# Block-causal attention and a feed-forward on one core: the softmax constant added one column at a time

## The chip, the cores and the metric

The kernel runs on one core of one Trainium2 chip. The metric is the device time of one execution in microseconds. Before the change the median of three runs is 1260.88 us (1260.35 to 1262.1).

## The reference, cut to what matters

Eight batches of eight heads, 576 positions, head size 64. Attention with a mask over blocks of 64 positions, then a feed-forward on the 4608 rows of 512.

```python
def _attn_ref(q, k, v):
    scores = scale * np.matmul(q, k.transpose(0, 1, 3, 2))
    scores = np.where(block_i >= block_j, scores, -1000000000.0)
    scores = scores - np.max(scores, axis=-1, keepdims=True)
    attn = np.exp(scores)
    attn = attn / (np.sum(attn, axis=-1, keepdims=True) + 1e-09)
    return np.matmul(attn, v)

def _moe_ref(x, w_in, w_out):
    h = x @ w_in
    g = np.where(h >= 1, h, np.where(h <= -1, 0.0, (h + 1) ** 2 / 4))
    return g @ w_out
```

The change touches the `+ 1e-09` and the sum before it.

## The kernel before, in words

Two heads make a *pair*; there are 32 pairs, four to a batch. The 576 query positions of a head are four tiles of 128 rows and a rest of 64. `scores(j, g)` handles the query tiles of head j of the pair in three groups: group 0 holds two tiles (128 and 256 keys wide) in one PSUM bank, groups 1 and 2 one tile each (384 and 512 keys). `scores_last` handles the two rests of a pair together, as 128 rows of 576 keys in two halves of 288.

Each group goes through the same steps. TensorE makes the scores `ps_s` (L483, L486). VectorE takes the negative row maximum `nm` (L506). ScalarE takes the exponential into `pr` (L510), and an accumulator read that follows puts each row's sum into one column of `sm`. VectorE then adds EPS to the sums (L492), inverts them (L493), both in `inverse`, and scales `pr` by the result (L516). In group 0 `sm` has two columns, so L492 and L493 work on 128x2 values, elsewhere on 128x1. In `scores_last` the two halves' sums are added first (L540), then comes `inverse` on one column, then the scaling (L542). The scaled `pr` goes through a DMA on SyncE's queue into `prr` (L250; in the second batch into other buffers, L246, and in the first straight from `pr`) and is turned by TensorE (`turn`, `turn_last`: L553 and L555 into `ps_t`), cut into two words by ScalarE and VectorE (L546, L548), and multiplied with V (L592 into `ps_av`). From the third batch on, `add_words` puts that result together: ScalarE copies half of it into `xtmp` (L614), VectorE adds the other half into `x` (L615). The queries and keys of the next pair are turned by TensorE into `ps_qk` (L402, L443) and cut into words by ScalarE and VectorE (L389, L390, L395, L396, L447).

`ps_s`, `ps_t`, `ps_av` and `ps_qk` all take their PSUM bank from `work_bank`: three banks in turn once the feed-forward runs. A matmul into a fresh bank therefore waits until the last reader of the bank's tile three turns earlier is done.

The feed-forward runs a chunk of 512 rows behind the attention, interleaved with it: `ffn_in` (L771, 12 matmuls into `ph`, then ScalarE L780, VectorE L781 and L784, ScalarE L785, GpSimd L786, which makes `gl`) and `ffn_out` (L795, L800). GpSimd also makes the second words of V (L380), of `x` (L658) and, in the first part of the program, of the weights (L183, L187, an in-order list of conversions) and of the keys (L365).

The source gives a list of steps, and a scheduler of the framework lays each engine's instructions out in an order of its own from the dependences and its estimates of durations. Each engine then runs its list in order, and waits on semaphores of the others. A change of a few instructions can so change the order of others.

Of the kernel before, what the change touches and what calls it, by code (L numbers as in the profile page):

```python
# [11 lines left out]
ALU = mybir.AluOpType  # L12
# [11 lines left out]
def block_attn_then_ffn(  # L24
# [9 lines left out]
    nc = tc.nc  # L34
# [19 lines left out]
    EPS = 1e-9  # L54
# [22 lines left out]
    def work_bank(name):  # L77

        banks["n"] += 1
        if banks["free"] and banks["n"] % 2:  # L80
            return ps_o.tile([P, 512], F32, tag="po", name=name)
        return ps_w.tile([P, 512], F32, tag="work", name=name)
# [23 lines left out]
    def last_blocks(t_):  # L106
# [19 lines left out]
        out=msel[:NTL, : NTL * BLK].rearrange("p (t c) -> p t c", c=BLK),  # L126
# [106 lines left out]
    def as_float32r(src, plain):  # L233

        if plain:
            wide = src.shape[1] > RING - 2 * S
            places = SPARE_WIDE if wide else SPARE
            moved = [places[spare[wide] % len(places)]]
            spare[wide] += 1
            if src.shape[1] > TCH:  # L240
                if "end" not in spare:
                    spare["end"] = att1.tile([P, G0 + P], F32R, tag="pa11", name="pre")[:, :BLK]
                moved.append(spare["end"])
            for i, dst in enumerate(moved):
                n = min(TCH, src.shape[1] - i * TCH)
                nc.sync.dma_start(dst[:, :n].bitcast(F32), src[:, i * TCH : i * TCH + n])  # L246
            return moved
        n, moved = src.shape[1], []
        wide = wide_tile(F32R, "prr")
        nc.sync.dma_start(wide[:, :n].bitcast(F32), src)  # L250
        for c0 in range(0, n, TCH):
            moved.append(wide[:, c0 : min(c0 + TCH, n)])
        return moved


    class Pair:
# [232 lines left out]

        def inverse(self, total):  # L490

            nc.vector.tensor_scalar_add(total, total, EPS)  # L492
            nc.vector.reciprocal(total, total)  # L493

        def scores(self, j, g):
# [23 lines left out]
        def scores_last(self):  # L519

            half = S // 2
            pr = att3.tile([P, S], F32, tag="pr", name="pr")
            nm = small.tile([P, 3], F32, tag="nm", name="nm")
            sm = small.tile([P, 3], F32, tag="sm", name="sm")
            banks = []
            for i in range(2):
                ps = work_bank("ps_s")
                for j in range(2):
                    self.product(ps[:, :half], j, SM, i * half, half, j == 0, j == 1)
                nc.vector.tensor_reduce(  # L530
                    out=nm[:, i : i + 1], in_=ps[:, :half], axis=AX.X, op=ALU.max, negate=True
                )
                banks.append(ps)
            nc.vector.tensor_tensor(out=nm[:, 2:3], in0=nm[:, 0:1], in1=nm[:, 1:2], op=ALU.min)
            for i in range(2):
                nc.scalar.activation(
                    pr[:, i * half : (i + 1) * half], banks[i][:, :half], AF.Exp,
                    bias=nm[:, 2:3], scale=1.0, accum_out=sm[:, i : i + 1],
                )
            nc.vector.tensor_tensor(out=sm[:, 2:3], in0=sm[:, 0:1], in1=sm[:, 1:2], op=ALU.add)  # L540
            self.inverse(sm[:, 2:3])
            nc.vector.tensor_scalar_mul(pr, pr, sm[:, 2:3])  # L542
            self.pr["last"] = as_float32r(pr, self.plain) if self.hop else [pr]

# [341 lines left out]
```

## Time and profile before

| | us |
|---|---|
| median of the runs (1260.35 to 1262.1) | 1260.88 |
| span of the profiled execution, first to last instruction | 1262.2 |
| TensorE busy in the span | 1193.1 (95%) |
| VectorE busy | 888.1 (70%) |
| ScalarE busy | 695.3 (55%) |
| GpSimd busy | 375.3 (30%) |

The page gives for the profiled execution its span, and no other time of its own; it is 1.3 us above the median of the runs. The program has three parts: a start of about 265 us in which the weights are converted and the first two batches go through attention; a body from 265 to 1064 us in which 24 pairs follow each other every 33.5 us, with the feed-forward between them; and an end of 198 us of feed-forward alone. In the rows of the profile PE is TensorE's matmul, PEld its weight load, DVE VectorE, ACT ScalarE, POOL GpSimd and SP SyncE; a row of the timeline has the start, the duration, engine, line, operation, what it writes and reads, and in square brackets the idle time ahead of it and what ended that.

### The profile page before, as it was taken

To read this page: it belongs to the slowest core of one execution; us is meant where nothing else is said; L and a number is where in the kernel's file an instruction comes from. 1 tells how busy PE (TensorE), PEld (TensorE's weight loads), DVE (VectorE), ACT (ScalarE), POOL (GpSimd) and SP (SyncE) were. 2 spreads that over 40 slices of the span, in tenths; PEclk is the share of its full clock that TensorE was granted. 3 is DMA by queue.
4 is the path that set the end of the run, shared out by engine and by line. 5 is a ranking of instruction groups with operands and counts; after the bars stand their busy time and mean duration, and the time that the engine had idled before them with its cause. 6 is when DMAs were issued, how large, how long until landed. Compare 5 with 4: busy or idle time off the path is not lost.

```text
span 1262.2 us, 19823 instructions
## 1 busy us (share of the span) xinstructions
PE 1193.1 (95%) x6280; PEld 995.7 (79%) x6280; DVE 888.1 (70%) x2092; ACT 695.3 (55%) x1731; POOL 375.3 (30%) x366
## 2 busy tenths in 40 slices
PE   4887988999999999999999999999999999999998
PEld 3665876788888888888888888888888888888886
DVE  8888688658777877787777877787778776222322
ACT  5776666446565666565556565565656655222222
POOL 3444556312222222222222222222222222222222
PEclk9887999999999999999999999999999999999999
DMA  5566676778887654565555545554556433422432
GB/s 162 167 183 208 215 253 213 217 219 236 277 270 242 187 151 146 163 195 158 148 151 174 179 144 156 153 179 140 161 156 188 143 118 119 133 93 91 134 101 100
DMA packets 177191, 215.39 MB, mean 171 GB/s; under 512 B 109872, under 2 KB 128304, under 8 KB 176320
## 3 DMA queue, kind: packets, MB, share of 16 engines
q1 hardware_dynamic: 177088, 214.14, 55.3%
q8 instruction: 50, 0.82, 0.3%
q14 instruction: 53, 0.43, 0.1%
HBM read 134.74 MB, written 31.98 MB: 132 GB/s over the span
## 4 chain that ended last, share of the span: by engine, by line
PE 69%; DVE 17%; ACT 5%; issue 5%; DMA 3%; POOL 1%; SPq 0%; ACTq 0%; DVEq 0%; POOLq 0%
PE ph L771 27%; PE po L795 15%; PE po L800 8%; PE ps_av L592 8%; PE ps_s L483 4%; PE ps_s L486 3%; ACT pr L510 3%; PE ps_t L553 2%; DVE pr L516 2%; DVE t L781 2%; DVE pb L548 2%; DVE t L784 2%; ACT t L780 2%; DVE nm L506 2%; DVE sm L492 1%
## 5 line engine op out<-in xcount | busy, mean ns | idle before, releaser
L786 POOL TENSOR_TENSOR gl<-t,gh 128x512 fp32r<-128x512 f32 x144 | 186.1, 1292 | 530.9 <-ACT gh L785 360.6
L795 PE MATMUL po<-wo,gh 128*128 128x512 f32 x1152 | 295.2, 397 | 0.1
L795 PEld LDWEIGHTS po<-wo,gh 128*128 128x128 f32 x1152 | 211.9, 189 | 43.6 <-ACT gh L785 0.6
L771 PE MATMUL ph<-xh,wih 128*128 128x512 f32 x576 | 231.4, 402 | 4.7 <-DVE t L784 4.4
L771 PE MATMUL ph<-xh,wil 128*128 128x512 f32 x576 | 226.8, 394 | 0.0
L771 PE MATMUL ph<-xl,wih 128*128 128x512 f32 x576 | 226.1, 393 | 0.0
L781 DVE SCALAR_TENSOR_TENSOR t<-t 128x512 f32<-128x512 f32 x144 | 101.8, 707 | 162.6 <-ACT t L780 159.6
L510 ACT ACTIVATE pr<-ps_s,nm 128x128 f32<-128x128 f32 (+3 forms) x256 | 133.9, 526 | 83.8 <-DVE nm L506 81.2
L780 ACT ACTIVATE t<-ph 128x512 f32<-128x512 f32 x144 | 85.9, 597 | 158.1 <-PE ph L771 158.1
L785 ACT CAST gh<-t 128x512 fp32r<-128x512 f32 x144 | 89.5, 621 | 121.0 <-DVE t L784 120.7
L800 PE MATMUL po<-wo,gl 128*128 128x512 f32 x576 | 155.4, 392 | 0.0
L483 PE MATMUL ps_s<-ka,qa 68*128 68x288 f32 (+4 forms) x384 | 134.7, 366 | 16.6 <-ACT pr L510 7.8
L506 DVE TENSOR_REDUCE nm<-ps_s 128x1 f32<-128x128 f32 (+3 forms) x256 | 119.0, 483 | 13.8 <-PE ps_s L486 12.9
L771 PEld LDWEIGHTS ph<-xh,wih 128*128 128x128 f32 x576 | 108.9, 189 | 24.2 <-DVE t L784 4.7
L771 PEld LDWEIGHTS ph<-xh,wil 128*128 128x128 f32 x576 | 108.8, 189 | 23.6
L800 PEld LDWEIGHTS po<-wo,gl 128*128 128x128 f32 x576 | 108.6, 189 | 22.9
L380 POOL TENSOR_TENSOR vsr<-vn,vsr 128x256 fp32r<-128x256 f32 (+1 forms) x96 | 56.4, 588 | 233.0 <-ACT vsr L379 232.0
L771 PEld LDWEIGHTS ph<-xl,wih 128*128 128x128 f32 x576 | 109.2, 190 | 19.3
L516 DVE TENSOR_SCALAR pr<-pr,sm 128x128 f32<-128x128 f32 (+3 forms) x256 | 118.4, 486 | 6.1 <-DMA ka<-kb 0.3
L486 PE MATMUL ps_s<-kb,qb 128*128 128x288 f32 (+4 forms) x384 | 120.9, 322 | 0.0
L492 DVE TENSOR_SCALAR sm<-sm 128x1 f32<-128x1 f32 (+1 forms) x224 | 55.8, 249 | 77.1 <-ACT pr L510 74.4
L784 DVE TENSOR_TENSOR t<-ph,t 128x512 f32<-128x512 f32 x144 | 98.7, 686 | 2.1
(111 smaller groups left out, 1811.9 us busy)
## 6 DMA issues: line engine op xcount, KB each, us to landing
wo<-wo_split SPq DMA_DIRECT2D x144, 512.0 KB, 3.4
prr<-pr SPq DMA_DIRECT2D x96, 192.0 KB, 2.5
prr<-pr SPq DMA_DIRECT2D x48, 256.0 KB, 2.6
out_dram<-ob SPq DMA_DIRECT2D x36, 256.0 KB, 2.3
bits<-in_moe_w_in_dram SPq DMA_DIRECT2D x16, 512.0 KB, 4.6
bits<-in_moe_w_out_dram SPq DMA_DIRECT2D x16, 512.0 KB, 4.0
wo_split<-ws SPq DMA_DIRECT2D x16, 512.0 KB, 3.0
qa<-qb SPq DMA_DIRECT2D x63, 128.0 KB, 2.4
```

The lines of the kernel that those rows point to most:

```text
L483: nc.tensor.matmul(ps, qa[:KA, j, c0 : c0 + P], ka[:KA, j, k0 : k0 + n], start=first, stop=False)
L486: nc.tensor.matmul(ps, qb[:, j, c0 : c0 + P], kb[:, j, k0 : k0 + n], start=False, stop=last)
L506: nc.vector.tensor_reduce(out=nm[:, i : i + 1], in_=ps[:, cs], axis=AX.X, op=ALU.max, negate=True)
L510: nc.scalar.activation(pr[:, cs], ps[:, cs], AF.Exp, bias=nm[:, i : i + 1], scale=1.0, accum_out=sm[:, i : i + 1],)
L516: nc.vector.tensor_scalar_mul(pr[:, cs], pr[:, cs], sm[:, i : i + 1])
L771: nc.tensor.matmul(ph, w[:, cc, fs], x[:, cc, xs], start=(cc == 0 and i == 0), stop=(cc == NCC - 1 and i == 2),)
L780: nc.scalar.activation(t_, ph, AF.Relu, bias=0.5, scale=0.5)
L781: nc.vector.scalar_tensor_tensor(out=t_, in0=t_, scalar=1.0, in1=t_, op0=ALU.min, op1=ALU.mult)
L784: nc.vector.tensor_tensor(out=t_, in0=ph, in1=t_, op=ALU.max)
L786: nc.gpsimd.tensor_tensor(out=gl, in0=t_, in1=gh.bitcast(F32), op=ALU.subtract)
L795: nc.tensor.matmul(po[tt], gh[:, ts_], wo[:, w, :], start=(fc == 0 and w == 0), stop=False)
L800: nc.tensor.matmul(po[tt], gl[:, ts_], wo[:, 0, :], start=False, stop=fc == NFC - 1)
```

## The change

EPS is added to the sums one column at a time: in group 0 of `scores` two instructions of 128x1 stand where one of 128x2 stood; the other groups have one column and one instruction as before. In `scores_last` one instruction adds the two halves' sums and EPS, where two did; it takes the second sum as a scalar per row.

```diff
         def inverse(self, total):
-            nc.vector.tensor_scalar_add(total, total, EPS)
+            for i in range(total.shape[1]):
+                nc.vector.tensor_scalar_add(total[:, i : i + 1], total[:, i : i + 1], EPS)
             nc.vector.reciprocal(total, total)
...
-            nc.vector.tensor_tensor(out=sm[:, 2:3], in0=sm[:, 0:1], in1=sm[:, 1:2], op=ALU.add)
-            self.inverse(sm[:, 2:3])
+            nc.vector.tensor_scalar(
+                out=sm[:, 2:3], in0=sm[:, 0:1], scalar1=sm[:, 1:2], scalar2=EPS,
+                op0=ALU.add, op1=ALU.add,
+            )
+            nc.vector.reciprocal(sm[:, 2:3], sm[:, 2:3])
             nc.vector.tensor_scalar_mul(pr, pr, sm[:, 2:3])
```

There are 64 group 0 and 32 calls of `scores_last`, so VectorE has 64 instructions more and 32 fewer. In the changed file the addition is L493, the reciprocal L494 (in `scores_last` L545), the scaling L517, the sum of the halves L541, and what stands behind them is four lines lower than before (L615 is L619, L555 is L559).

In the body, VectorE's order around group 0 of the first head of a pair, before:

```order
L506 TENSOR_REDUCE nm<-ps_s 128x1 x2
L615 TENSOR_TENSOR x_7454<-ps_av,xtmp 64x256
L492 TENSOR_SCALAR sm<-sm 128x2
L493 RECIPROCAL sm<-sm 128x2
L615 TENSOR_TENSOR x_7454<-ps_av,xtmp 64x256
L516 TENSOR_SCALAR pr<-pr,sm 128x128
L516 TENSOR_SCALAR pr<-pr,sm 128x256
```

Around group 0 of the second head, on the same engine, after the change:

```order
L507 TENSOR_REDUCE nm<-ps_s 128x1 x2
L390 SCALAR_TENSOR_TENSOR qb<-ps_qk,qb 64x512
L493 TENSOR_SCALAR sm<-sm 128x1 x2
L494 RECIPROCAL sm<-sm 128x2
L517 TENSOR_SCALAR pr<-pr,sm 128x128
L517 TENSOR_SCALAR pr<-pr,sm 128x256
L396 TENSOR_TENSOR kb<-ps_qk,kb 64x512
L552 TENSOR_TENSOR pb_9951<-ps_t,pb_9950 128x4x128
L507 TENSOR_REDUCE nm<-ps_s 128x1
```

At both places the one 128x2 addition has become two of 128x1 where it stood, each with a wait of its own for ScalarE's sum, and nothing else has moved; in the body TensorE's and GpSimd's orders are as before.

In the start the scheduler has moved more. TensorE's order in the first pairs, before:

```order
L486 MATMUL ps_s<-kb,qb 128x512
L555 MATMUL ps_t<-ident_r,pr 128x128 x3
L592 MATMUL ps_av<-pa_235,vs 128x256
L592 MATMUL ps_av<-pa_235,vs 128x128
L592 MATMUL ps_av<-pa_236,vs 128x256
L555 MATMUL ps_t<-ident_r,pr 128x128 x3
L592 MATMUL ps_av<-pa_236,vs 128x128
L423 MATMUL ps_qk<-ident_r,qs 128x128 x4
```

and after:

```order
L486 MATMUL ps_s<-kb,qb 128x512
L559 MATMUL ps_t<-ident_r,pr 128x128
L596 MATMUL ps_av<-pa_236,vs 128x256
L559 MATMUL ps_t<-ident_r,pr 128x128 x2
L596 MATMUL ps_av<-pa_236,vs 128x128
L559 MATMUL ps_t<-ident_r,pr 128x128 x3
L423 MATMUL ps_qk<-ident_r,qs 128x128 x4
L423 MATMUL ps_qk<-ident_r,ks 128x128 x4
L596 MATMUL ps_av<-pa_237,vs 128x256
```

Turns and products of the first two batches change places there, and so do GpSimd's conversions and SyncE's transfers beside them.

## The prediction

> **What bounds the kernel now.** I read the page first, then the busy times by stretch, then who waited for whom in the body, then the two places there at which TensorE waits. The stretches, with the columns PE, PEld, DVE, ACT, POOL, granted clock, DMA share, GB/s:
>
> ```profile
> 0.00:122.00 122.00, 85.05 (x441) 67.94 (x441) 106.12 (x279) 83.19 (x218) 49.35 (x52) 0.91 0.60 175
> 122.00:265.00 143.00, 131.37 (x657) 106.17 (x658) 106.17 (x223) 88.50 (x205) 70.66 (x61) 0.96 0.73 229
> 265.00:1064.00 799.00, 783.69 (x4322) 662.14 (x4321) 620.99 (x1507) 475.15 (x1227) 209.12 (x219) 1.00 0.58 175
> ```
>
> In the body (third row) TensorE is busy 98%, so only its idle time can be won: 799 − 783.7 = 15.3 us by the modelled ends, at full clock. In the first 122 us it idles 37 us, and VectorE is busy 87%. The waits of the body (total, times, longest) name two causes:
>
> ```profile
> PE ps_s L483 <- ACT pr L510: 7.8, 24, 0.4
> PE ps_qk L443 <- DVE x L615: 6.9, 19, 0.4
> ```
>
> Together 14.7 us, nearly all of the idle time. There are 24 pairs in the body, so each pair loses time at these two places. Neither names the lines that change; whether they lead back to them is read from the timeline. First VectorE's groups, the body alone (busy us, mean ns, idle before):
>
> ```profile
> L492 DVE TENSOR_SCALAR sm<-sm 128x2 f32<-128x2 f32 x48 | 26.0, 542 | 26.0 <-ACT pr L510 26.0
> L492 DVE TENSOR_SCALAR sm<-sm 128x1 f32<-128x1 f32 x119 | 18.2, 153 | 40.2 <-ACT pr L510 37.8
> L493 DVE RECIPROCAL sm<-sm 128x2 f32<-128x2 f32 x48 | 8.0, 166 | 1.6
> L540 DVE TENSOR_TENSOR sm<-sm 128x1 f32<-128x1 f32 x24 | 3.8, 160 | 27.4 <-ACT pr L536 27.4
> ```
>
> The addition on two columns takes 542 ns, on one 153 ns; one element more is no reason for that. The timeline of one pair, at group 0 of the first head (place 1):
>
> ```profile
> 603.51 1.29 POOL L786 TENSOR_TENSOR gl<-t,gh 128x512 fp32r<-128x512 f32 x1 [0.98 <-ACT gh L785]
> 604.11 0.20 ACT L510 ACTIVATION_READ_ACCUMULATOR pr<-ps_s,nm 128x1 f32 x1
> 604.34 0.37 ACT L614 COPY xtmp<-ps_av 64x256 f32<-64x256 f32 x1
> 604.34 0.49 DVE L492 TENSOR_SCALAR sm<-sm 128x2 f32<-128x2 f32 x1 [0.77 <-ACT pr L510]
> 604.37 0.46 PE L553 MATMUL ps_t<-ident_r,prr 128*128 128x128 f32 x4
> 604.67 0.41 PE L483 MATMUL ps_s<-ka,qa 68*128 68x384 f32 x1
> 604.87 0.17 DVE L493 RECIPROCAL sm<-sm 128x2 f32<-128x2 f32 x1
> 604.92 0.34 PE L486 MATMUL ps_s<-kb,qb 128*128 128x384 f32 x1
> 605.06 0.43 DVE L615 TENSOR_TENSOR x<-ps_av,xtmp 64x256 f32<-64x256 f32 x1
> 605.64 0.25 PE L443 MATMUL ps_qk<-ident_r,qk 128*128 128x128 f32 x1 [0.38 <-DVE x L615]
> ```
>
> GpSimd's L786 ends at 604.80 and the addition at 604.83: it is held until GpSimd is done. The reciprocal, L615 and TensorE's L443 follow in a chain. At group 0 of the second head (place 2) the same happens, 621.87 against 621.89:
>
> ```profile
> 620.59 1.28 POOL L786 TENSOR_TENSOR gl<-t,gh 128x512 fp32r<-128x512 f32 x1 [5.78 <-issue]
> 621.31 0.58 DVE L492 TENSOR_SCALAR sm<-sm 128x2 f32<-128x2 f32 x1 [0.27 <-ACT pr L510]
> 622.13 0.55 DVE L516 TENSOR_SCALAR pr<-pr,sm 128x128 f32<-128x128 f32 x2
> 622.72 0.69 DVE L396 TENSOR_TENSOR kb<-ps_qk,kb 64x512 fp32r<-64x512 f32 x1
> 623.44 0.69 DVE L548 TENSOR_TENSOR pb<-ps_t,pb 128x512 fp32r<-128x512 f32 x1
> 624.05 0.55 DVE L506 TENSOR_REDUCE nm<-ps_s 128x1 f32<-128x384 f32 x1
> 624.53 0.52 PE L553 MATMUL ps_t<-ident_r,prr 128*128 128x128 f32 x5
> 624.63 0.58 ACT L510 ACTIVATE pr<-ps_s,nm 128x384 f32<-128x384 f32 x1 [2.13 <-DVE nm L506]
> 625.11 0.19 ACT L510 ACTIVATION_READ_ACCUMULATOR pr<-ps_s,nm 128x1 f32 x1
> 625.36 0.50 PE L483 MATMUL ps_s<-ka,qa 68*128 68x512 f32 x1 [0.30 <-ACT pr L510]
> ```
>
> Behind the held addition VectorE runs without idle time (no bracket) to the row maximum at 624.05; ScalarE has waited 2.13 us for that; its exponential frees the bank for which TensorE waits at 625.36. So both of TensorE's waits hang on L492's hold.
>
> **Are single columns held?** And is what comes next? Rows with GpSimd at work beside VectorE:
>
> ```profile
> 309.50 1.29 POOL L786 TENSOR_TENSOR gl<-t,gh 128x512 fp32r<-128x512 f32 x1 [0.60 <-ACT vsr L379]
> 310.21 0.15 DVE L492 TENSOR_SCALAR sm<-sm 128x1 f32<-128x1 f32 x1 [0.39 <-ACT pr L510]
> ...
> 166.00 1.04 POOL L183 TENSOR_TENSOR bits<-bits 128x512 int32<-128x512 int32 x1 [0.63 <-DVE sm L492]
> 166.38 0.15 DVE L493 RECIPROCAL sm<-sm 128x2 f32<-128x2 f32 x1
> ...
> 229.04 1.31 POOL L187 TENSOR_TENSOR ws<-bits,ws 128x512 fp32r<-128x512 f32 x1
> 229.22 1.47 DVE L516 TENSOR_SCALAR pr<-pr,sm 128x128 f32<-128x128 f32 x2
> ```
>
> One column: 0.15 us in the middle of L786, not held. The two-column reciprocal: not held. The scaling L516 is held: its two instructions end at 230.69, 0.34 after GpSimd's 230.35.
>
> **The change, part by part.** *Place 1.* The first column's sum is there before the second's, and VectorE has been idle 0.77 us, so the added instruction is hidden. The second column starts at 604.34 as before and ends at 604.49. The reciprocal follows 0.04 later (as 604.83 to 604.87), at 604.53, and L615 0.19 after that, 604.72; but L615 needs `xtmp`, ready at 604.71, so I take 604.74. That is 0.32 earlier than 605.06. TensorE could start L443 0.25 after L486 (as L486 came 0.25 after L483, which is as wide), at 605.17; it will start at 605.32 instead of 605.64. All 0.32 is won and 0.15 remains. What is late next is ScalarE's copy. Where the wait is short already (24 − 19 = 5 pairs) I take 0.25: 19 × 0.32 + 5 × 0.25 = 7.3 us.
>
> *Place 2.* The second column ends at 621.46 and the reciprocal starts at 621.50; the scaling comes at 621.70 and is itself held until 621.87. By the row at 229.22 its pair ends 0.34 later, at 622.21, against 622.68 before: 0.47 won, because the reciprocal now runs inside the hold. L396, L548 and L506 follow 0.47 earlier, ScalarE is idle, and its accumulator read ends at 624.83 instead of 625.30. TensorE is then free at 624.53 + 5 × 0.075 = 624.90 (four turns took 604.37 to 604.67), so L483 starts 0.45 earlier and waits no more: 24 × 0.45 = 10.8 us. From below: if the scaling's hold ate all but the reciprocal's 0.19, 24 × 0.19 = 4.6.
>
> *The sum of the halves.* One 160 ns addition becomes none, 24 times in the body and 8 in the start. L540 has idle time before it, and the scaling ends 0.19 earlier; no wait of TensorE in the body names its transfer, so it is worth nothing there. The fused form isn't in the trace: between 153 ns, the one-column addition, and 542, a held one; I take 153, since it too writes one column. At worst the difference, 0.4, lies in VectorE's idle time.
>
> *The start.* The 16 group 0 there cost 16 × 0.19 more, 8 calls of `scores_last` 8 × 0.19 less: 1.5 us on a VectorE busy 87%. Against that stand holds that go:
>
> ```profile
> L492 DVE TENSOR_SCALAR sm<-sm 128x2 f32<-128x2 f32 x16 | 5.6, 353 | 5.8 <-ACT pr L510 5.8
> L540 DVE TENSOR_TENSOR sm<-sm 128x1 f32<-128x1 f32 x8 | 3.1, 382 | 1.2 <-ACT pr L536 1.1
> PE ps_t L555 <- DVE sm L492: 6.7, 2, 4.0
> ```
>
> 353 and 382 ns against 150 make 16 × 0.2 + 8 × 0.2 = 5 us, of which the scaling behind inherits most. I count zero. The moved orders of TensorE, GpSimd and SyncE decide more: one such wait as in the last row is 4.0 us (the other 2.7), and one may appear or vanish. Hence ±5 us.
>
> *The end* is unchanged. Sum: −7.3 − 10.8 = −18.1 us. The profiled span of 1262.2 would become 1244.1; its 1.3 us above the median I carry along: 1260.9 − 18.1 = 1242.8.
>
> [...]
>
> **Rivals.** *The hold moves on whole*: at place 2 the scaling inherits it and the chain gains nothing. Only place 1 is won: 1260.9 − 7.3 = 1253.6. For it: L516 is held at 229.22. Against it: the reciprocal's share, and the fact that only 0.17 us of GpSimd's run is left when the scaling comes.
>
> *Single columns are held like the pair*: the second column, at 604.34 and 621.31, ends with GpSimd as now, and the body keeps its time: 1260.9. Against it stands the row at 310.21 and the mean of 153 over 119, which leaves no room for holds. [...]
>
> *Slower: the additional instruction lies on the path and no hold goes.* If the 542 ns were not GpSimd's doing but the price of two columns, the split would add 0.19 at 48 places: +9.1, 1270. It decides where GpSimd's run ends less than 0.19 after the addition's start; here it ends 0.46 and 0.56 after. A start that loses over 20 us would do the same; five waits of 4.0 us are needed for that.
>
> **How the numbers follow.** Both holds shortened: 0.74, with 1237 to 1249 for itself (±5 of the start, and place 1 may close fully). Only place 1: 0.17. No effect: 0.04. Slower by either way: 0.05. Faster than 0.2% (2.5 us, about what a measurement here can tell) takes the first two: 0.91. The range must reach the second case: 1236 to 1256.
>
> **What would show it.** Right: L493 at 128x1 near 153 ns with no 128x2 left; TensorE's wait at L443 (same line after) down from 0.38 to about 0.06 by the modelled ends; that of L483 on L510 nearly gone; the body 18 us shorter; GpSimd's L786 (now L790) still 1.29. The first scaling of the second head should be longer than 0.29, ending soon after GpSimd. Wrong: new TensorE waits on transfers or on `gl` in the body, where it would run 2% ahead of its suppliers, or a start of more than 270 us.

## The result and the profile after

| | before | after |
|---|---|---|
| median of the runs, us | 1261.49 (1260.35 to 1268.99, 4 runs) | 1245.87 (1244.16 to 1246.8, 4 runs) |
| span of the profiled execution | 1262.2 | 1242.4 |
| first L443 of the body | 266.06 | 264.18 |
| body, first to last L443 of its 24 pairs | 775.34 | 757.51 |
| from there to the end | 220.76 | 220.69 |

The ratio of the runs is 0.9858 (95% interval 0.983 to 0.9886): the change made the kernel 1.4% faster. The forecast was 1242.8 with 1236 to 1256. Of the 19.8 us between the two profiled executions 17.8 lie in the body and 1.9 in the start.

The busy times after, by stretch (columns as before):

```profile
0.00:122.00 122.00, 85.04 (x450) 67.66 (x451) 106.22 (x288) 84.72 (x219) 49.93 (x53) 0.94 0.61 181
122.00:265.00 143.00, 132.66 (x658) 106.30 (x657) 100.37 (x226) 89.58 (x208) 69.57 (x60) 0.95 0.71 225
265.00:1064.00 799.00, 797.88 (x4417) 677.53 (x4416) 612.91 (x1543) 481.70 (x1235) 212.99 (x221) 1.00 0.58 177
```

In the third stretch, which now also holds some 20 us of the end, TensorE idles 1.1 us by the modelled ends, where it was 15.3. VectorE's groups over the whole program:

```profile
L493 DVE TENSOR_SCALAR sm<-sm 128x1 f32<-128x1 f32 x256 | 38.5, 151 | 72.2 <-ACT pr L511 68.9
L494 DVE RECIPROCAL sm<-sm 128x2 f32<-128x2 f32 x64 | 10.5, 164 | 1.8
L541 DVE TENSOR_SCALAR sm<-sm 128x1 f32<-128x1 f32 x32 | 6.8, 213 | 28.6 <-ACT pr L537 28.6
```

The additions take 151 ns on average and none over 157, though 163 of the 256 start while GpSimd is at work. Place 1 of one pair in the timeline after:

```profile
593.98 1.29 POOL L790 TENSOR_TENSOR gl<-t,gh 128x512 fp32r<-128x512 f32 x1 [0.98 <-ACT gh L789]
594.35 0.15 DVE L493 TENSOR_SCALAR sm<-sm 128x1 f32<-128x1 f32 x1 [0.32 <-ACT pr L511]
...
594.80 0.37 ACT L618 COPY xtmp<-ps_av 64x256 f32<-64x256 f32 x1
594.81 0.15 DVE L493 TENSOR_SCALAR sm<-sm 128x1 f32<-128x1 f32 x1 [0.30 <-ACT pr L511]
...
595.00 0.17 DVE L494 RECIPROCAL sm<-sm 128x2 f32<-128x2 f32 x1
595.20 0.43 DVE L619 TENSOR_TENSOR x<-ps_av,xtmp 64x256 f32<-64x256 f32 x1
595.38 0.34 PE L486 MATMUL ps_s<-kb,qb 128*128 128x384 f32 x1
595.77 0.25 PE L443 MATMUL ps_qk<-ident_r,qk 128*128 128x128 f32 x1
```

Both additions run in the middle of GpSimd's instruction (593.98 to 595.27) and are not held; the first sits in time in which VectorE idles. L443 now starts 0.39 after L486, where it was 0.72 (605.64 − 604.92). Place 2:

```profile
610.71 1.29 POOL L790 TENSOR_TENSOR gl<-t,gh 128x512 fp32r<-128x512 f32 x1 [5.78 <-issue]
611.20 0.39 DVE L493 TENSOR_SCALAR sm<-sm 128x1 f32<-128x1 f32 x2
611.63 0.17 DVE L494 RECIPROCAL sm<-sm 128x2 f32<-128x2 f32 x1
611.83 0.55 DVE L517 TENSOR_SCALAR pr<-pr,sm 128x128 f32<-128x128 f32 x2
...
613.74 0.55 DVE L507 TENSOR_REDUCE nm<-ps_s 128x1 f32<-128x384 f32 x1
614.65 0.51 PE L557 MATMUL ps_t<-ident_r,prr 128*128 128x128 f32 x5
614.80 0.19 ACT L511 ACTIVATION_READ_ACCUMULATOR pr<-ps_s,nm 128x1 f32 x1
615.05 0.50 PE L483 MATMUL ps_s<-ka,qa 68*128 68x512 f32 x1
```

From the five turns to L483 it is 0.40 (615.05 − 614.65), where it was 0.83 (625.36 − 624.53), and the bracket on L483 is gone. ScalarE's accumulator read ends at 614.99, about when TensorE is free.

### The profile page after: what moved, and what is told of

It is laid out like the page before. It is cut to its first block, busy times and chain, and to the rows that moved or that the text cites. A ratio compares the mean times of both kernels' runs of the same rounds, so it can differ in the third digit from the quotient of the medians.

```text
span 1242.4 us, 19859 instructions
## 1 busy us (share of the span) xinstructions
PE 1188.9 (96%) x6280; PEld 994.1 (80%) x6280; DVE 866.5 (70%) x2124; ACT 697.5 (56%) x1731; POOL 373.8 (30%) x366
## 4 chain that ended last, share of the span: by engine, by line
PE 81%; DVE 4%; DMA 4%; POOL 2%; ACT 2%; issue 1%; SPq 0%; ACTq 0%; POOLq 0%; DVEq 0%
PE ph L775 30%; PE po L799 20%; PE po L804 10%; PE ps_av L596 8%; PE ps_s L483 5%; PE ps_s L486 4%; PE ps_t L557 4%; DMA bits<-in_moe_w_in_dram 1%; PE ps_qk L402 1%; DMA wo_split<-ws 1%; DMA bits<-in_moe_w_out_dram 1%; POOL bits L183 1%; DVE bits L177 1%; DMA vsr<-pr 1%; DVE nm L507 0%
## 5 line engine op out<-in xcount | busy, mean ns | idle before, releaser
L483 PE MATMUL ps_s<-ka,qa 68*128 68x288 f32 (+4 forms) x384 | 135.1, 367 | 10.3 <-DMA ka<-mrow 4.0
L380 POOL TENSOR_TENSOR vsr<-vn,vsr 128x256 fp32r<-128x256 f32 (+1 forms) x96 | 56.5, 589 | 224.6 <-ACT vsr L379 223.3
L486 PE MATMUL ps_s<-kb,qb 128*128 128x288 f32 (+4 forms) x384 | 120.9, 322 | 0.0
L517 DVE TENSOR_SCALAR pr<-pr,sm 128x128 f32<-128x128 f32 (+3 forms) x256 | 116.5, 476 | 5.6
L493 DVE TENSOR_SCALAR sm<-sm 128x1 f32<-128x1 f32 x256 | 38.5, 151 | 72.2 <-ACT pr L511 68.9
```

Source lines behind the costliest of these rows:

```text
L483: nc.tensor.matmul(ps, qa[:KA, j, c0 : c0 + P], ka[:KA, j, k0 : k0 + n], start=first, stop=False)
L486: nc.tensor.matmul(ps, qb[:, j, c0 : c0 + P], kb[:, j, k0 : k0 + n], start=False, stop=last)
L517: nc.vector.tensor_scalar_mul(pr[:, cs], pr[:, cs], sm[:, i : i + 1])
```

## The experiments

In each the body is measured as in the table, first to last L443. That is the number that separates the theories: every edit also makes the scheduler lay the first 265 us out anew, and the start then moves by a few us whatever the edit is for. The runs share executions of the kernel before, with medians of 1263 to 1265 us in these comparisons.

**The split alone.** The diff's first hunk; the halves are summed and inverted as before.

> The body is measured from L443 of the first to L443 of the last of its 24 pairs, 23 steps: 775.3 us before (266.06 to 1041.40), 757.5 after (264.18 to 1021.69). Hold theory (two-column addition held by GpSimd's instruction): the split alone gives all of the body's gain, 757.5 within 1; total 1243 to 1248. Rival, the fused sum of the halves counts: the body stays nearer 775. Rival, the moved orders of the start count: the body keeps 775 and the first L443 comes elsewhere than 266.

Measured: body 757.95, first L443 at 268.52, 1248.54 us (ratio 0.9875, 0.9856 to 0.9894). The split alone gives the body's whole gain. The start is 4.3 us later than after the full change.

**The fused sum alone.** The diff's second hunk.

> Only the sum of the halves is fused. Hold theory: both additions of a pair are held as before (mean 0.54 us in the body), body 775.3 within 1, total 1256 to 1265 with the start's moved order. Rival, fusion counts: body well below 775, at best 32 x 0.19 = 6 us of VectorE less.

Measured: body 774.93, first L443 at 267.59, 1266.86 us (ratio 1.0023, 1.0007 to 1.004). Waits and groups in its body:

```profile
PE ps_s L483 <- ACT pr L510: 7.8, 24, 0.4
PE ps_qk L443 <- DVE x L618: 6.9, 20, 0.4
```
```profile
L492 DVE TENSOR_SCALAR sm<-sm 128x2 f32<-128x2 f32 x46 | 24.8, 540 | 24.3 <-ACT pr L510 24.3
L540 DVE TENSOR_SCALAR sm<-sm 128x1 f32<-128x1 f32 x23 | 4.9, 214 | 26.3 <-ACT pr L536 26.3
```

Both waits stand as before. The fused instruction takes 214 ns, not the 153 that the prediction took for it, and the body is none the longer for it; VectorE idles ahead of it. By itself this half gains nothing in the body, and its start came 1.5 us later.

**One place at a time.** The changed kernel, with the addition left on two columns for the second head, or for the first:

```diff
-            self.inverse(sm[:, :m])
+            self.inverse(sm[:, :m], j == 0)   # one column at a time if true; the other run: j == 1
```

> The changed kernel with the two-column addition kept for the second head. Hold theory: place 1 alone is won, 0.32 a pair: body 775.3 - 23 x 0.32 = 768; TensorE's wait at L483 on L510 stays at 0.30 and that at L443 falls to 0.06. If the two places are not independent (the second takes back what the first gives): 775, or 757 if the first alone was the cause.

> The changed kernel with the two-column addition kept for the first head. Hold theory: place 2 alone is won, 0.45 a pair: body 775.3 - 23 x 0.45 = 765; TensorE's wait at L443 stays at 0.38. Rival, the hold moves on to the scaling whole: place 2 gives nothing, body 775.

Measured: first head alone, body 767.32, 1257.71 us (ratio 0.9948, 0.993 to 0.9967); second head alone, body 765.13, 1255.35 us (0.9927, 0.991 to 0.9943). The wait that remains in the body of the first, with its held addition:

```profile
PE ps_s L483 <- ACT pr L512: 7.5, 23, 0.4
...
L494 DVE TENSOR_SCALAR sm<-sm 128x2 f32<-128x2 f32 x23 | 13.6, 589 | 6.1 <-ACT pr L512 6.1
```

and of the second:

```profile
PE ps_qk L443 <- DVE x L620: 6.9, 19, 0.4
PE ps_s L483 <- ACT pr L512: 0.2, 1, 0.2
...
L494 DVE TENSOR_SCALAR sm<-sm 128x2 f32<-128x2 f32 x24 | 11.9, 495 | 18.9 <-ACT pr L512 18.9
```

Each head's addition carries one of TensorE's two waits and not the other. Place 1 is worth 8.0 us and place 2 10.2, over 23 steps; together 18.2 against 17.8 for both, so the two are independent. The rival that the hold moves on whole to the scaling is out: place 2 was won.

**What is held: three columns in one instruction.** The sums of group 0 lie in a tile of three columns, the third a spare, and `tensor_scalar_add(sm[:, :3], sm[:, :3], EPS)` adds once.

> The changed kernel, but group 0 adds EPS in one instruction over three columns (the third is a spare that nothing reads); the reciprocal still takes two. It asks whether one column goes free because its count is odd, or because it is one. If any odd count goes free: mean about 0.155 us in the body, body 757.5 or a little less. [...] If the price were per column and no hold: 0.54 x 3/2, body well above 775.

Measured: body 774.69, 1267.77 us (ratio 1.0037, 1.0021 to 1.0054).

```profile
L524 DVE TENSOR_SCALAR sm<-sm 128x3 f32<-128x3 f32 x46 | 24.7, 537 | 24.4 <-ACT pr L519 24.4
PE ps_qk L448 <- DVE x L629: 6.6, 19, 0.4
```

Three columns are held like two, 537 ns against 542; an odd count is no way out, and the price does not go by columns. In the body each of them ends 0.02 to 0.03 us after a GpSimd instruction. One column in the same form takes 151 ns in the changed kernel.

**What it is held by: GpSimd's subtraction in two halves.** The kernel before, with L786 as two instructions of 256 columns.

> The kernel before, additions as before, but GpSimd's subtraction gl (L786) in two instructions of 256 columns, some 0.74 us each by the row of L380, instead of one of 1.29. Hold theory, if VectorE gets in between the two: at place 2 the first half ends about where the addition starts (621.33 and 621.31), so it takes 0.15 to 0.2 instead of 0.58; at place 1 the first half ends at 604.25, before the addition at 604.34, which then waits for the second half to 605.0: 0.65 instead of 0.49. Body about 775.3 + 23 x (0.16 - 0.4) = 770. If nothing gets in between: held to the end of the second half, later than before at both places, body over 775. Rival, two columns cost 0.54 by themselves: durations unchanged, body 775.

Measured: body 782.27, 1272.96 us (ratio 1.0067, 1.0046 to 1.0088). Place 2 of one pair:

```profile
621.52 1.44 POOL L787 TENSOR_TENSOR gl<-t,gh 128x256 fp32r<-128x256 f32 x2 [5.65 <-issue]
622.25 0.74 DVE L492 TENSOR_SCALAR sm<-sm 128x2 f32<-128x2 f32 x1 [0.27 <-ACT pr L510]
```

The two halves end at 622.96 and the addition at 622.99, 0.74 long instead of 0.58: its end has moved with GpSimd's, 0.03 behind it as before (621.87 and 621.89). Whether VectorE gets in between two GpSimd instructions is not answered here: the second half starts at 622.22, ahead of the addition, and so it is in every pair of the body. The kernel before has it both ways. At 294.59 a scaling of 512 columns starts beside L786, which ends at 295.83; the next GpSimd instruction (L380) has already started at 295.79 and ends at 296.29, and the scaling ends at 296.11, after 1.52 us instead of 0.49. It is held through the first alone. At 444.98 a scaling of 512 columns starts 0.22 us before a GpSimd instruction ends (L380, at 445.20); the next one (L658) has already started at 445.16 and ends at 446.58, and the scaling ends at 446.87, after 1.89 us instead of 0.49. It is held through both.

That two columns cost 0.54 by themselves is ruled out by the kernel before as well. Of its 64 two-column additions nine start while GpSimd is idle, and take 0.15 to 0.17 us. The other 55 take 0.27 to 1.02, and each ends 0.02 to 0.03 us after a GpSimd instruction.

Longer on GpSimd is longer in the body, where both waits of TensorE grew, from 0.38 and 0.30 in the pair of the prediction to:

```profile
606.57 0.25 PE L443 MATMUL ps_qk<-ident_r,qk 128*128 128x128 f32 x1 [0.56 <-DVE x L615]
...
626.44 0.50 PE L483 MATMUL ps_s<-ka,qa 68*128 68x512 f32 x1 [0.47 <-ACT pr L510]
```

**Fewer instructions: no EPS.** The additions are left out altogether, and L541 only adds the halves; this part of the computation is missing (the sums are at least 1, the row's largest exponential).

> EPS is left out altogether: no addition before the reciprocal, 256 VectorE instructions fewer than after, and the halves are only added. Hold theory: at place 1 L615's successor waits for ScalarE's copy xtmp anyway, at place 2 TensorE no longer waits; the body gains nothing, 757 within 1, and the total moves only with the start, 1240 to 1249. Rival, the additions lie on the path: 23 x 2 x 0.19 = 8.7 us less in the body, 749.

Measured: body 768.19, first L443 at 260.06, 1251.59 us (ratio 0.9908, 0.989 to 0.9926). The body is neither 757 nor 749. Place 1 shows why:

```profile
593.64 1.30 POOL L788 TENSOR_TENSOR gl<-t,gh 128x512 fp32r<-128x512 f32 x1 [0.98 <-ACT gh L787]
594.47 0.17 DVE L492 RECIPROCAL sm<-sm 128x2 f32<-128x2 f32 x1 [0.78 <-ACT pr L509]
594.67 0.61 DVE L515 TENSOR_SCALAR pr<-pr,sm 128x128 f32<-128x128 f32 x2
595.31 0.43 DVE L617 TENSOR_TENSOR x<-ps_av,xtmp 64x256 f32<-64x256 f32 x1
595.88 0.25 PE L443 MATMUL ps_qk<-ident_r,qk 128*128 128x128 f32 x1 [0.50 <-DVE x L617]
```

The scheduler has put both scalings ahead of the addition into `x` here, in the body, where the other edits had left the order alone. The first starts within GpSimd's run (until 594.94), and L617 comes behind both. The wait at L443 is 0.50, longer than the 0.38 before the change; TensorE's wait at L483 is gone but for 0.5 us in the whole body, so place 2 stays won. The expectation missed this because it took the order for given. Once in four pairs TensorE's and ScalarE's instructions of the feed-forward change places too.

**The changed kernel again, and what is late next.** The changed kernel unaltered, and with the second head's copy into `xtmp` made by VectorE:

```diff
-            nc.scalar.copy(xtmp[main, :n], ps[rest, :])
+            if c0 == 0 and j == 1:
+                nc.vector.tensor_copy(xtmp[main, :n], ps[rest, :])
+            else:
+                nc.scalar.copy(xtmp[main, :n], ps[rest, :])
```

> The changed kernel once more, unaltered, beside the next two on the same chip. Every theory: body 757.5 within 0.5; the start as in the first profile, 264 within 2, if it is set by the order of instructions and not by chance.

> The changed kernel, but the second head's copy into xtmp (L618, columns 0 to 255) is made by VectorE, ahead of the additions, in the time in which VectorE idles for the sums, not by ScalarE behind the exponentials. If ScalarE's copy is what is late next at place 1, as the prediction says: L443 no longer waits, 0.2 a pair less, body 757.5 - 23 x 0.2 = 753, VectorE 24 x 0.42 = 10 us busier at no cost. If something else holds L443 (TensorE's own pace, the bank's other readers): 757.5. If VectorE's 0.42 pushes the scaling past its transfer's time: over 757.5.

Measured: unaltered, body 757.87, first L443 at 266.10, 1246.16 us (ratio 0.9866, 0.9844 to 0.9887). With the copy moved, body 752.79, first L443 at 263.49, 1239.95 us (0.9814, 0.9788 to 0.9839). Place 1 there:

```profile
591.56 0.42 DVE L619 COPY xtmp<-ps_av 64x256 f32<-64x256 f32 x1
592.01 0.15 DVE L493 TENSOR_SCALAR sm<-sm 128x1 f32<-128x1 f32 x1
592.20 0.43 DVE L622 TENSOR_TENSOR x<-ps_av,xtmp 64x256 f32<-64x256 f32 x1
592.65 0.15 DVE L493 TENSOR_SCALAR sm<-sm 128x1 f32<-128x1 f32 x1
592.84 0.17 DVE L494 RECIPROCAL sm<-sm 128x2 f32<-128x2 f32 x1
592.87 0.34 PE L486 MATMUL ps_s<-kb,qb 128*128 128x384 f32 x1
593.05 0.23 PE L443 MATMUL ps_qk<-ident_r,qk 128*128 128x128 f32 x1
```

L443 follows L486 by 0.18: TensorE no longer waits, and the body is 757.5 − 752.8 = 4.7 us shorter, 5.1 against the run beside it. That the copy alone was late, as the prediction said, is not shown. The scheduler has also put the addition into `x` ahead of the second EPS addition and the reciprocal, as the rows show; in the changed kernel it stood behind them. There the copy and the reciprocal both ended at 595.17, and L619 came 0.03 later. That is so in 23 of the body's pairs (L619 comes 0.03 to 0.04 behind either), so by these rows to take away one of the two would have gained next to nothing. This run took both away.

The same program began its body at 264.18 in one profiled execution and at 266.10 in the other. The row of the second for the first 122 us:

```profile
0.00:122.00 122.00, 86.63 (x441) 69.51 (x442) 104.44 (x286) 84.08 (x218) 48.64 (x52) 0.88 0.59 176
```

The granted clock there was 0.88, against 0.94 in the first. The four compute engines' orders in the start are the same in both. So 2 us of the start can differ between executions without any change of order.

**Both together.** The copy moved, EPS left out, and the scaling of the first head's group 0 written behind the second addition into `x`, so that the order of the no-EPS run does not come back.

> The same with EPS left out, and with the first head's group 0 scaled behind the second add into x: 256 VectorE instructions fewer. With both holds out of TensorE's way the body cannot gain by it: 753 within 1. The scaling at place 2 comes 0.2 sooner and is held for that much longer by GpSimd, so nothing is lost either. The start decides the total, 1236 to 1245.

Measured: body 750.98, first L443 at 262.19, 1235.38 us (ratio 0.9779, 0.9755 to 0.9804), the fastest of all. At place 1 the order held: the scaling stands behind the addition into `x`. The body is 1.8 us shorter than with the copy alone, where none was expected beyond 1. Of that, 1.1 us lies in the first step and every fourth after it, just those in which TensorE's order in the feed-forward has changed, as it had in the run without EPS; whether that is the cause was not tried.

## Why the prediction was right, point by point

*Both waits hang on the held addition.* Shown: with both held additions split the wait at L483 is gone and that at L443 is down to 0.08 us a pair at most, where about 0.06 was forecast; with one addition split one of the two goes.

*Place 1, 0.32 a pair, 7.3 us.* Measured 0.33 in the pair shown and 8.0 us with the first head alone. The wait was short in six pairs, not five (0.11 to 0.15 us); L443 comes 0.27 to 0.31 sooner behind L486 there, so the 0.25 was a little too cautious. The first pair of the body had no wait, and nothing was won at it. Over all pairs L443 comes 7.3 us sooner behind L486; where the rest of the 8.0 lies is not shown. What is late next was named as ScalarE's copy alone; after the change the reciprocal ends with it.

*Place 2, 0.45 a pair, 10.8 us.* Measured 0.43 in the pair shown and 10.2 us with the second head alone. One step of its working was off: the scaling was to be held until GpSimd's end and to finish 0.34 after it. It started at 611.83 with GpSimd running until 612.00 and took 0.55, as long as without GpSimd, and the first of its two instructions took 0.286, not the longer time that the prediction named as a sign. The traces show why: the held scalings of 128 columns ended 0.08 to 0.09 after GpSimd (nine in the kernel before), and this one's own 0.286 already reached 0.12 past it. In the run without EPS, where 0.26 was left, it took 0.345 and ended 0.08 after. The pair ended 0.38 after GpSimd instead of 0.34, so the sum hardly moved.

*The sum of the body, 18.1 us.* Measured 17.8 and 17.5 in the two executions, over the 23 steps between 24 pairs; the sum counted 24 gains.

*The fused sum is worth nothing in the body.* Right, 774.93 against 775.34, though the instruction takes 214 ns and not 153.

*The start counts zero, ±5.* 264.18 and 266.10 against 266.06, and 260 to 268.5 over the other edits that moved its order. Its terms were not tested one by one, so that the start came out near zero is luck within the stated ±5. Why one order is better than another there was not tried either; the difference of 4.3 us between the split alone and the full change lies in it, and by the repeated run some 2 us of such a difference can come without a change of order.

*Why 1245.9 and not 1242.8.* The base was off, and not a term of the sum. Wherever both are recorded, an execution's time is 1.65 to 1.85 us above its own span (1244.16 against 1242.4). The profiled span of 1262.2 before so belongs to an execution of about 1263.9, an estimate by that difference, and the three runs whose median the forecast starts from were about 3 us faster than that. The 1.3 us that the prediction carried along compared different executions. From the medians of 1263.3 to 1265.0 that the kernel before has in the later comparisons the same sum gives 1245.2 to 1246.9; the profiled span was forecast at 1244.1 and came at 1242.4 and 1244.7.

*The added instructions.* VectorE runs 32 instructions more (2124 against 2092), yet its busy time fell from 888.1 to 866.5 us. Some 17 us of that lies in the additions of EPS themselves, whose holds went: 224 of them took 55.8 us, 31.6 of it in the 64 on two columns, and 256 of one column take 38.5, 151 ns each.

## What to carry to other kernels

Where a tiny instruction takes several times what a neighbour of nearly the same form takes (542 ns against 153 here), lay its end beside the ends of the other engines' instructions: here ends 0.02 to 0.03 us apart named the holder, and the cost was read from who stands behind the held instruction, not from its busy time. Look for a form that is not held before moving work to another engine; here it was one column, at 153 ns beside GpSimd and 148 without, and at place 1 the one more instruction (594.35, 0.15 us) lay in time in which VectorE idled. And look at the order again after each edit: when the additions were taken out, the scheduler put longer instructions ahead of the one that TensorE waits for, and all of one place's gain was lost.

## What the runs showed of the hardware beyond the expected

The held instructions of these runs ended shortly after GpSimd's: in the kernel before 0.02 to 0.03 us for the 55 additions on two columns, 0.08 to 0.09 for nine scalings of 128 columns. A scaling of 128 columns that started 0.17 us before GpSimd's end, with 0.286 of its own, was not lengthened (611.83 in the changed kernel), while additions that started 0.46 and 0.56 before it were (604.34 and 621.31 in the kernel before). Where a second GpSimd instruction had started before the first ended, the hold of a scaling of 512 columns went through both at one place (444.98, 1.89 us) and through the first alone at another (294.59, 1.52 us); what decides it was not shown. One column did not go free in every form: in the start of the kernel before, two of the additions of the halves' sums (L540, 128x1, two tiles as inputs) start beside GpSimd, at 49.94 and 95.66; they take 1.38 and 0.75 us, where the 30 others, which start with GpSimd idle, take 0.15 to 0.16, and end 0.02 after it. The fused form, one tile and a scalar per row, was not held at two such places: in the run of the fused sum alone two of them start less than 0.1 us after a GpSimd instruction of over 1 us has begun (L365 at 50.00, as beside the addition at 49.94, and L183 at 116.45), and take 0.20 and 0.21. At two places it was GpSimd's instruction that took longer: in the start of the kernel before two scalings of 384 columns (112.51 and 189.14) take 0.40 and 0.41, no more than the usual 0.42, beside a GpSimd instruction that had started 0.11 and 0.52 before them (L365 and L183), while that instruction takes 2.16 and 1.82 us instead of the 1.41 and 1.04 usual at its line; whether the scaling is the cause was not tried. The clock granted in the first 122 us of the changed kernel was 0.94 in one execution and 0.88 in the other.
